# Attention and gated MLP on one core: a third open VectorE exponential, a later read of its scores, and a VectorE queue planned without the drain

## The chip, the cores and the metric

The kernel runs on one core of one Trainium2 chip. The metric is the device time of one execution in microseconds, smaller is better. Three runs of the kernel before took 938.67, 939.95 and 939.96 us; their median is 939.95 us.

## The reference

The input is one sequence of 2048 rows of 640 numbers in bf16. A layer norm without weights is followed by attention with 32 heads of 20 columns, an output projection and a residual sum; then a second layer norm, a gated MLP of width 1728 without a nonlinearity (the gate is multiplied with the up projection), a down projection and another residual sum.

```python
h  = x + A(layernorm(x))
h2 = h + B(layernorm(h))
# A: q, k, v = split(x @ wqkv);  p = softmax(q k^T * 20**-0.5);  (p v) @ wo
# B: ((x @ w_gate) * (x @ w_up)) @ w_down
```

The softmax has 32 x 2048 x 2048 exponentials, and they are the bulk of the work.

## The kernel before

**Units and tiles.** The scores are computed transposed, keys on the 128 partitions and queries along the row. A unit is one head, 128 keys and 512 queries: a 128x512 block of scores, one PSUM bank. Three units make a score tile `sc` of 128x1536 (three banks); there are two such tiles, used in turn. TensorE fills one with three matmuls (line 490), ScalarE takes the exponential of the whole tile into a bf16 tile `E` (line 503), and TensorE multiplies the values with E and sums into `acc` (line 677). Tile i can be filled only when tile i - 2 has been read. There are 683 tiles. Four heads form a group g, 512 queries a pass ("0" to "3"; the last pass is cut in two halves of 256, "A" and "B", for six of its eight groups). One group in one pass is a segment: 64 units, 21.3 tiles. In pass "0" the first four groups are cut in chunks by keys, since keys and values are still being made; all later segments are of the kind "only".

**VectorE's exponentials.** In some tiles ScalarE does only the first 1024 columns, and VectorE computes the exponential of the third unit with four instructions on 128x512: a read of the scores out of PSUM into `xv` (line 528), two polynomial steps into `xt` (lines 537 and 538) and a last step into `xe` (line 533), whose 16-bit integers are the bits of a bf16 number. The first instruction is issued in `emit_x`; the other three go on a list, `x_open`, and are issued one by one wherever the plan sees room on VectorE. A unit is open from its read until its last step. `xv` and `xt` have two buffers each, `xe` has six (X_OUT). A finished unit waits in its `xe` buffer until line 677 has used it; `x_live` counts the units between their read and that use.

**The order of the work is computed while the program is built.** Each engine executes its instructions in the order of the program, so the kernel carries a plan with a clock for each engine in ns: `at["pe"]` for TensorE, `at["exp"]` for the end of ScalarE's last exponential, `at["dve"]` for the time at which VectorE can take another instruction, `at["mi"]` for when the one bank `mi` that all other matmuls share is free, `at["slot"]` for when each score tile is free. A loop over the tiles (line 1206) issues the tile's score matmuls and its exponential (`emit_S`), multiplications with values (`emit_AV`), and then pieces of other jobs (projections, output projection, the MLP) as long as TensorE has time before the next scores are due (`run_job`). If there is no job it issues two matmuls that nobody reads (`keep_warm`, line 463). Every evacuation from PSUM goes through `dve(ns)`, which first lets `spare(ready)` issue waiting VectorE work (steps of open units, layer-norm pieces in `aux`), and then charges ns to `at["dve"]`; ready is `at["pe"]` plus LAT, 150 ns. The charges are about the recorded durations: 690 for a 128x512 evacuation, 490 for 320 columns. A step of an open unit is charged 605, or 720 when the instruction just before it belonged to the same unit. `spare(until)` issues work as long as its cost ends no later than `until` plus TOL, 200 ns.

**Who takes a unit.** `x_takes(i)` (line 514) lets VectorE take the third unit of tile i if the tile is full, lies in one segment of the kind "only" and in a pass before the last (or there are no jobs at all), at least three tiles of the segment follow, fewer than two units are open, `at["dve"]` is less than TOL after `at["pe"]`, and fewer than six units are live. `emit_S` asks only if ScalarE is planned to be busy when the scores are ready. The three conditions at the end are what the change touches:

```python
and len(x_open) < 2 and at["dve"] < at["pe"] + TOL and len(x_live) < X_OUT
```

At the end of a segment `emit_AV` calls `need_x(s)`, which issues all steps still open for that segment before the values of the next one begin. The sum `acc` is then evacuated (line 688), its reciprocal row sums go through DRAM, and GpSimd multiplies (line 600).

Of the kernel before, what the change touches and what calls it, by code (L numbers as in the profile page):

```python
# [11 lines left out]
F32 = mybir.dt.float32  # L12
# [7 lines left out]
P = 128  # L20
# [16 lines left out]
BANK = 512  # L37
# [17 lines left out]
WARM, LEAD = 58, 3  # L55
LAG = 10
EXP_NS, EXP_END, EXP_COL = 50, 166, 5 / 6
S_NS, S_EXP, SWITCH, LAT = 323, 500, 110, 150
TOL, LEAST, MARGIN = 200, 430, 100
WO_NS, SUMS_NS, ROOT_NS, ROWS_NS = 1500, 6000, 5000, 5000  # L60
END_OF_TIME = 10 ** 9
X_LEAST, X_OUT, X_SOON = 3, 6, 4
E_BUFS = 6
SHIFT = 544.0
LOG2E = 1.4426950408889634
# [12 lines left out]
def kernel(  # L78
# [25 lines left out]
    xp = pool("xp")  # L104
# [134 lines left out]
    def dve(ns):  # L239
        ready = at["pe"] + LAT  # L240
        spare(ready)
        x_last[0] = None
        at["dve"] = max(at["dve"], ready) + ns

    def apply1(t, m32, r, k, eng=None):
        eng = eng or nc.vector
# [139 lines left out]
    def step():  # L386
        if cur["fresh"] and (first() or waiting):
            if cur["gen"] is not None:
                jobs.appendleft((cur["key"], cur["gen"]))
            cur["key"], cur["gen"] = (urgent if first() else waiting).popleft()  # L390
        c = advance()
        if c == WAIT:
            waiting.append((cur["key"], cur["gen"]))
            cur["gen"] = None
            c = advance() if jobs and jobs[0][0][0] == "y" else NEXT
        if c is None:
            return None
        if c == FREE:
            advance()
            return FREE  # L400
        if cur["fresh"] and c not in (END, NEXT):
            at["pe"] = max(at["pe"], at["mi"] if cur["key"] != ON_ACC else 0) + SWITCH
        cur["fresh"] = c in (END, NEXT)
        if cur["fresh"]:
            if cur["key"] != ON_ACC:
                at["mi"] = max(at["mi"], at["dve"] + LAT)
        else:
            at["pe"] += c
        return c
# [31 lines left out]
    def spare(until):  # L441
        while True:
            soon = x_open and last_tile[x_open[0][0]] - now["i"] <= X_SOON
            if at["dve"] + (x_next()[0] if soon or x_open and not aux else 600) > until + TOL:
                break
            if soon:
                step_x()
            elif not step_aux() and not step_x():
                break
# [30 lines left out]
    def emit_S(i):  # L480
        sc = scp.tile([P, EW], F32, name="sc")
        us, n = tiles[i]
        for s, kt, j, _ in us:
            p, g = segs[s][0:2]
            ensure(("k", g, kt // TPB))
            ensure(("q", PASS[p][0], g))
        for s, kt, j, o in us:
            p, g = segs[s][0:2]
            b, c0, w = PASS[p]
            nc.tensor.matmul(  # L490
                sc[:, o:o + w],
                lhsT=kT[g][SLOT * j:SLOT * (j + 1), kt * P:(kt + 1) * P],
                rhs=q_of(g, b, c0, w)[SLOT * j:SLOT * (j + 1), :],
                start=True, stop=True)
        begin = max(at["pe"], at["slot"][-2])
        at["pe"] = begin + S_NS
        start = max(at["exp"], begin + S_EXP)
        n_act, took = n, None
        if start == at["exp"] and x_takes(i):
            n_act = n - BANK  # L500
            took = emit_x(sc[:, n_act:n], [(s, kt, j, o - n_act) for s, kt, j, o in us if o >= n_act])
        e = ep.tile([P, EW], BF16, name="E")
        exps = nc.scalar.activation(e[:, 0:n_act], sc[:, 0:n_act], ACT.Exp, bias=EXP_BIAS, scale=SM_SCALE)  # L503
        if took is not None:
            tc.declare_no_dep(exps.ins, took.ins, reason="both only read the score tile, in different banks")
        run = EXP_NS + n_act * EXP_COL
        free = start + run + EXP_END
        at["slot"].append(free if took is None else max(free, at["dve"] + LAT))
        at["exp"] = start + run
        for s, kt, j, o in us:  # L510
            if o < n_act:
                av_q.append((i, s, kt, j, e[:, o:o + PASS[segs[s][0]][2]]))

    def x_takes(i):
        us, n = tiles[i]
        s = us[-1][0]
        return (n == EW and segs[s][4] == "only" and (PASS[segs[s][0]][0] < LAST_B or not jobs and not cur["gen"]) and last_tile[s] - i >= X_LEAST and len({u[0] for u in us}) == 1
                and len(x_open) < 2 and at["dve"] < at["pe"] + TOL and len(x_live) < X_OUT)

    def emit_x(ps, us):  # L520
        s = us[0][0]
        w = PASS[segs[s][0]][2]
        v = xp.tile([P, BANK], F32, name="xv", bufs=2)
        u = v[:].bitcast(U16).rearrange("p (n h) -> p n h", h=2)[:, :, 0]
        t = xp.tile([P, BANK], F32, name="xt", bufs=2)
        e = xp.tile([P, BANK], I16, name="xe", bufs=X_OUT)
        dve(690)
        took = nc.vector.tensor_scalar(v[:], ps, X_SCALE, X_BASE, ALU.mult, ALU.max)  # L528
        x_live.append((s, us[-1][1], us[-1][2]))
        x_left[s] = x_left.get(s, 0) + 1  # L530

        def last():
            nc.vector.scalar_tensor_tensor(e[:], t[:], X_R, v[:], ALU.mult, ALU.add)  # L533
            x_left[s] -= 1
            x_put.append([(now["i"], s, kt, j, e[:, o:o + w].bitcast(BF16)) for s, kt, j, o in us])
        x_open.append((s, deque([
            lambda: nc.vector.scalar_tensor_tensor(t[:], u, X_P, u, ALU.add, ALU.mult),  # L537
            lambda: nc.vector.scalar_tensor_tensor(t[:], t[:], X_Q, u, ALU.add, ALU.mult),  # L538
            last])))
        x_last[0] = x_open[-1]  # L540
        return took
# [103 lines left out]
    def emit_AV(upto):  # L645
        put_x()
        if not av_q:
            return
        if acc["seg"] is not None and av_q[0][1] != acc["seg"]:
            need_x(acc["seg"])  # L650
            put_x()
        s = av_q[0][1]
        p, g, lo, hi, kind = segs[s]
        b, c0, w = PASS[p]
        if acc["seg"] != s:
            if at["pe"] < at["acc"] and now["i"] < acc["from"] and min(u[0] for u in av_q) > now["i"] - E_BUFS:
                return
            acc["seg"], acc["left"], acc["n"] = s, (hi - lo) * HPG, [0] * HPG
            acc["t"] = accp.tile([P, QB], F32, name="acc")
        most, rows = 2 * HPG * QB // w, [[] for _ in range(HPG)]  # L660
        for u in av_q:
            if u[0] > upto or u[1] != s:
                break
            if len(rows[u[3]]) < most // HPG:
                rows[u[3]].append(u)
        ready = sum(len(r) for r in rows)
        if ready < min(most, acc["left"]) and min(u[0] for u in av_q) > upto - 3:
            return
        for u in [r[k] for k in range(most // HPG) for r in rows if k < len(r)]:
            av_q.remove(u)  # L670
            _, _, kt, j, e = u
            x_used.add((s, kt, j))
            while x_live and x_live[0] in x_used:
                x_live.popleft()
            ensure(("v", kt, g // (NG // 2)))
            h = HPG * g + j
            nc.tensor.matmul(  # L677
                acc["t"][SLOT * j:SLOT * (j + 1), 0:w],
                lhsT=vx[kt][:, VS * h:VS * h + SLOT], rhs=e,
                start=(acc["n"][j] == 0), stop=(acc["n"][j] == hi - lo - 1))  # L680
            acc["n"][j] += 1
        acc["left"] -= ready
        at["pe"] += SWITCH + -(-ready // HPG) * w * 5 // 12
        if acc["left"] == 0:
            dve(690)
            if kind in ("copy", "only"):
                asb = parts[g] if kind == "copy" else nrm.tile([P, QB], F32, name="asb")
                nc.vector.tensor_copy(asb[:, 0:w], acc["t"][:, 0:w])
                if kind == "copy":
                    part[g] = asb  # L690
            else:
                asb = part[g]
                nc.vector.tensor_tensor(asb[:, 0:w], acc["t"][:, 0:w], asb[:, 0:w], ALU.add)
            acc["seg"], acc["from"], at["acc"] = None, now["i"] + 2, at["dve"] + LAT
            if s == FINAL:
                final["asb"] = asb
            elif (p, g) in FAST:
                opens["nf", p, g] = at["dve"] + LAT
                urgent.append((("nf", p, g), job_norm(s, asb)))
            elif kind in ("only", "last"):  # L700
                norm(s, asb)
# [640 lines left out]
```

## Time and profile before

| what | value |
|---|---|
| median of three runs | 939.95 us |
| the profiled execution's own time | 938.44 us |
| its span, first to last instruction | 936.4 us |
| granted TensorE clock, mean | 0.993 |
| busy: ScalarE | 887.8 us (95%) |
| busy: TensorE | 818.6 us (87%) |
| busy: VectorE | 620.7 us (66%) |
| busy: GpSimd | 61.6 us (7%) |
| exponentials on ScalarE, 1536 columns | 555, mean 1536 ns |
| exponentials on ScalarE, 1024 columns | 128, mean 1123 ns |
| units on VectorE | 127 |

DVE is VectorE, ACT is ScalarE, PE is TensorE and POOL is GpSimd. A duration is what the profiler records from an instruction's start to its end; on ACT and on DVE the next instruction often starts before the recorded end of the one before, so the number that tells how fast an engine gets on is the distance between two starts. Of the 128 shorter exponentials 127 belong to tiles whose third unit VectorE took; the last is simply the last tile. The waits view lists who stood idle for whom, with the total, the number of times and the longest; an engine can only be late for another one through such a wait.

### The profile page before, as it was taken

How to read it: one execution, taken by the hardware profiler on the slowest of the kernel's cores; microseconds unless marked ns; L12 is line 12 of the kernel's file. 1: busy time of each engine (PE TensorE's matmuls, PEld its weight loads, DVE VectorE, ACT ScalarE, POOL GpSimd, SP SyncE). 2: the span in 40 equal slices, each digit the busy share in tenths (PEclk: the TensorE clock that was granted, in tenths of full speed). 3: DMA queues.
4: the chain of work that ended last, by engine and by line, in shares of the span. 5: the costliest groups of instructions: out<-in, count | busy, mean ns of one | idle time of the engine just before them, and what ended most of it. 6: DMA issues, size and time to landing. Idle time of an engine off the chain costs nothing.

```text
span 936.4 us, 18059 instructions
## 1 busy us (share of the span) xinstructions
PE 818.6 (87%) x7138; PEld 321.7 (34%) x7219; DVE 620.7 (66%) x1222; ACT 887.8 (95%) x719; POOL 61.6 (7%) x155
## 2 busy tenths in 40 slices
PE   8788888888987898998898898998888889978897
PEld 5233232222232222332233222332332334435565
DVE  7674359898888888887888888887562331133342
ACT  6999999999999999999999999999999999999941
POOL 3310011000000000000000000000000000000000
PEclk9999999999999999999999999999899999999999
DMA  6000010011150022014120312002402000212310
GB/s 190 29 2 1 1 27 25 13 35 27 41 164 7 27 77 63 13 34 169 56 57 2 91 48 62 20 29 62 120 2 70 15 12 20 64 28 56 78 43 18
DMA packets 67818, 44.44 MB, mean 47 GB/s; under 512 B 18504, under 2 KB 63404, under 8 KB 67728
## 3 DMA queue, kind: packets, MB, share of 16 engines
q1 hardware_dynamic: 67728, 43.23, 16.6%
q8 instruction: 58, 0.95, 0.4%
q14 instruction: 32, 0.26, 0.1%
HBM read 35.91 MB, written 7.30 MB: 46 GB/s over the span
## 4 chain that ended last, share of the span: by engine, by line
ACT 51%; PE 24%; issue 18%; DVE 7%; ACTq 0%
ACT E L503 51%; PE sc L490 5%; PE acc L677 4%; PE mi L980 3%; PE mi L1035 3%; PE mi L291 2%; PE f L980 2%; PE f L1035 1%; PE mi L305 1%; PE mi L463 1%; DVE xt L538 1%; DVE st L193 1%; DVE u L258 1%; DVE kT L298 1%; PE mi L998 1%
## 5 line engine op out<-in xcount | busy, mean ns | idle before, releaser
L503 ACT ACTIVATE E<-sc 128x1536 bf16<-128x1536 f32 (+1 forms) x683 | 870.3, 1459 | 8.8 <-PE sc L490 6.4
L490 PE MATMUL sc<-qa,kT 32*128 32x512 bf16 x1536 | 201.1, 384 | 47.5 <-ACT E L503 37.0
L490 PEld LDWEIGHTS <-kT 32*128 32x128 bf16 x2432 | 83.8, 91 | 282.8 <-issue 236.1
L677 PE MATMUL acc<-E,vx 128*32 128x512 bf16 (+1 forms) x2305 | 168.2, 351 | 0.5 <-ACT E L503 0.5
L528 DVE TENSOR_SCALAR xv<-sc 128x512 f32<-128x512 f32 x127 | 86.9, 688 | 32.3 <-PE sc L490 31.6
L538 DVE SCALAR_TENSOR_TENSOR xt<-xt,xv 128x512 f32<-128x512 f32 x127 | 92.6, 737 | 0.7
L533 DVE SCALAR_TENSOR_TENSOR xe<-xt,xv 128x512 int16<-128x512 f32 x127 | 90.8, 720 | 0.8
L291 PE MATMUL mi<-lnT,wp 128*128 128x512 bf16 x280 | 81.8, 381 | 10.4 <-DVE kT L298 3.8
L537 DVE SCALAR_TENSOR_TENSOR xt<-xv 128x512 f32<-128x512 uint16 x127 | 87.5, 704 | 0.3
L490 PE MATMUL sc<-qb,kT 32*128 32x256 bf16 (+1 forms) x896 | 69.1, 291 | 16.5 <-ACT E L503 13.3
L600 POOL TENSOR_TENSOR on<-asb,bc 128x512 bf16<-128x512 f32 (+1 forms) x30 | 36.5, 1216 | 694.6 <-DMA bc<-scr 547.7
L677 PEld LDWEIGHTS <-vx 128*32 128x32 bf16 x2432 | 44.4, 95 | 64.3 <-issue 63.8
L1035 PE MATMUL mi<-wd,hh 128*128 128x320 bf16 x364 | 64.3, 302 | 2.0 <-DVE xr L1039 2.0
L258 DVE CAST u<-mi 128x512 bf16<-128x512 f32 (+1 forms) x42 | 29.0, 690 | 36.1 <-PE mi L980 31.7
L1035 PEld LDWEIGHTS <-hh 128*128 128x128 bf16 x448 | 38.4, 97 | 39.9 <-issue 28.3
L980 PE MATMUL mi<-ln2T,wg 128*128 128x512 bf16 (+1 forms) x161 | 45.8, 382 | 6.9 <-DVE u L258 6.4
L463 PE MATMUL mi<-kT,ident 128*128 128x512 bf16 x151 | 48.6, 390 | 1.8 <-issue 0.5
L980 PE MATMUL mi<-ln2T,wu 128*128 128x512 bf16 (+1 forms) x157 | 45.2, 387 | 5.7 <-DVE hh L988 4.7
L988 DVE TENSOR_TENSOR hh<-mi,u 128x512 bf16<-128x512 f32 (+1 forms) x42 | 28.8, 685 | 25.4 <-PE mi L980 22.9
L291 PEld LDWEIGHTS <-wp 128*128 128x128 bf16 x310 | 25.0, 97 | 52.9 <-issue 39.1
L914 PE MATMUL mi<-wo,on 128*128 128x320 bf16 x224 | 38.6, 301 | 2.4 <-DVE xr L918 2.3
L298 DVE TENSOR_SCALAR kT<-mi,one_row 128x512 bf16<-128x512 f32 x30 | 22.4, 746 | 26.7 <-PE mi L291 26.5
(151 smaller groups left out, 582.6 us busy)
## 6 DMA issues: line engine op xcount, KB each, us to landing
bc<-scr SPq DMA_DIRECT2D x100, 64.0 KB
wu<-in_B_w_up_dram SPq DMA_DIRECT2D x20, 320.0 KB
wg<-in_B_w_gate_dram SPq DMA_DIRECT2D x20, 320.0 KB
qsp<-qa SPq DMA_DIRECT2D x8, 384.0 KB
xr<-in_A_x_dram SPq DMA_DIRECT2D x16, 160.0 KB
out_dram<-xr SPq DMA_DIRECT2D x14, 160.0 KB
wd<-in_B_w_down_dram SPq DMA_DIRECT2D x13, 160.0 KB
xs<-in_A_x_dram SPq DMA_DIRECT2D x3, 640.0 KB
```

Source lines behind the costliest of these rows:

```text
L291: nc.tensor.matmul(ps[:], lhsT=wslice(m, g, c), rhs=lnT[:, c, ch * QB:(ch + 1) * QB], start=(c == 0), stop=(c == KT - 1))
L463: nc.tensor.matmul(ps[:], lhsT=ident[:], rhs=kT[0][:, 0:BANK], start=True, stop=True)
L490: nc.tensor.matmul(sc[:, o:o + w], lhsT=kT[g][SLOT * j:SLOT * (j + 1), kt * P:(kt + 1) * P], rhs=q_of(g, b, c0, w)[SLOT * j:SLOT * (j + 1) ...
L503: exps = nc.scalar.activation(e[:, 0:n_act], sc[:, 0:n_act], ACT.Exp, bias=EXP_BIAS, scale=SM_SCALE)
L528: took = nc.vector.tensor_scalar(v[:], ps, X_SCALE, X_BASE, ALU.mult, ALU.max)
L533: nc.vector.scalar_tensor_tensor(e[:], t[:], X_R, v[:], ALU.mult, ALU.add)
L537: lambda: nc.vector.scalar_tensor_tensor(t[:], u, X_P, u, ALU.add, ALU.mult),
L538: lambda: nc.vector.scalar_tensor_tensor(t[:], t[:], X_Q, u, ALU.add, ALU.mult),
L677: nc.tensor.matmul(acc["t"][SLOT * j:SLOT * (j + 1), 0:w], lhsT=vx[kt][:, VS * h:VS * h + SLOT], rhs=e, start=(acc["n"][j] == 0), stop=(ac ...
L914: nc.tensor.matmul(ps[:, 0:HALF], lhsT=on[g][:, t * P:(t + 1) * P], rhs=wo[g][:, cs], start=(g == 0), stop=(g == NG - 1))
L980: nc.tensor.matmul(ps[0:M, 0:n], lhsT=st["w", fp][k][:, c, f2 * P:f2 * P + M], rhs=st["ln2T"][:, c, c0:c0 + n], start=(c == 0), stop=(c == ...
L1035: nc.tensor.matmul(ps[:, 0:HALF], lhsT=st["hh"][f][0:K, t * P:(t + 1) * P], rhs=late["Wd"][f][0:K, cs], start=(f == 0), stop=(f == 2 * FP ...
```

## The change

Five edits. (1) A constant DRAIN of 80 ns: `dve(ns)` charges 80 ns less to `at["dve"]`, and the places that use `at["dve"]` as the time when a result is there (for `mi`, for the score tile, for `acc`) add it back. (2) A third unit may be open, and `xv` and `xt` get a third buffer. (3) `xe` has five buffers in place of six, and at most four live units let another one be taken. (4) A new time `last_of_x`, the planned start of the tile's shortened exponential plus 50 + 1024 x 5/6 + 166 - 150 - 690 - 200, that is about 29 ns after the start: a unit may be taken if `at["dve"]` is less than that (or less than `at["pe"]` plus TOL, as before). (5) Before the unit is taken, `spare(last_of_x)` issues waiting VectorE work up to that time, so that the read of the scores stands behind it in VectorE's queue.

```diff
--- before.py
+++ after.py
@@ -55,11 +55,12 @@
 WARM, LEAD = 58, 3
 LAG = 10
 EXP_NS, EXP_END, EXP_COL = 50, 166, 5 / 6
-S_NS, S_EXP, SWITCH, LAT = 323, 500, 110, 150
+S_NS, S_EXP, SWITCH, LAT, DRAIN = 323, 500, 110, 150, 80
 TOL, LEAST, MARGIN = 200, 430, 100
 WO_NS, SUMS_NS, ROOT_NS, ROWS_NS = 1500, 6000, 5000, 5000
 END_OF_TIME = 10 ** 9
-X_LEAST, X_OUT, X_SOON = 3, 6, 4
+X_LEAST, X_OUT, X_SOON = 3, 5, 4
+X_READ, X_SLACK = 690, 200
 E_BUFS = 6
 SHIFT = 544.0
 LOG2E = 1.4426950408889634
@@ -240,7 +241,7 @@
         ready = at["pe"] + LAT
         spare(ready)
         x_last[0] = None
-        at["dve"] = max(at["dve"], ready) + ns
+        at["dve"] = max(at["dve"], ready) + ns - DRAIN
 
     def apply1(t, m32, r, k, eng=None):
         eng = eng or nc.vector
@@ -403,7 +404,7 @@
         cur["fresh"] = c in (END, NEXT)
         if cur["fresh"]:
             if cur["key"] != ON_ACC:
-                at["mi"] = max(at["mi"], at["dve"] + LAT)
+                at["mi"] = max(at["mi"], at["dve"] + DRAIN + LAT)
         else:
             at["pe"] += c
         return c
@@ -496,8 +497,10 @@
         at["pe"] = begin + S_NS
         start = max(at["exp"], begin + S_EXP)
         n_act, took = n, None
-        if start == at["exp"] and x_takes(i):
+        last_of_x = start + EXP_NS + (n - BANK) * EXP_COL + EXP_END - LAT - X_READ - X_SLACK
+        if start == at["exp"] and x_takes(i, last_of_x):
             n_act = n - BANK
+            spare(last_of_x)
             took = emit_x(sc[:, n_act:n], [(s, kt, j, o - n_act) for s, kt, j, o in us if o >= n_act])
         e = ep.tile([P, EW], BF16, name="E")
         exps = nc.scalar.activation(e[:, 0:n_act], sc[:, 0:n_act], ACT.Exp, bias=EXP_BIAS, scale=SM_SCALE)
@@ -505,26 +508,26 @@
             tc.declare_no_dep(exps.ins, took.ins, reason="both only read the score tile, in different banks")
         run = EXP_NS + n_act * EXP_COL
         free = start + run + EXP_END
-        at["slot"].append(free if took is None else max(free, at["dve"] + LAT))
+        at["slot"].append(free if took is None else max(free, at["dve"] + DRAIN + LAT))
         at["exp"] = start + run
         for s, kt, j, o in us:
             if o < n_act:
                 av_q.append((i, s, kt, j, e[:, o:o + PASS[segs[s][0]][2]]))
 
-    def x_takes(i):
+    def x_takes(i, last):
         us, n = tiles[i]
         s = us[-1][0]
         return (n == EW and segs[s][4] == "only" and (PASS[segs[s][0]][0] < LAST_B or not jobs and not cur["gen"]) and last_tile[s] - i >= X_LEAST and len({u[0] for u in us}) == 1
-                and len(x_open) < 2 and at["dve"] < at["pe"] + TOL and len(x_live) < X_OUT)
+                and len(x_open) < 3 and at["dve"] < max(last, at["pe"] + TOL) and len(x_live) < X_OUT)
 
     def emit_x(ps, us):
         s = us[0][0]
         w = PASS[segs[s][0]][2]
-        v = xp.tile([P, BANK], F32, name="xv", bufs=2)
+        v = xp.tile([P, BANK], F32, name="xv", bufs=3)
         u = v[:].bitcast(U16).rearrange("p (n h) -> p n h", h=2)[:, :, 0]
-        t = xp.tile([P, BANK], F32, name="xt", bufs=2)
+        t = xp.tile([P, BANK], F32, name="xt", bufs=3)
         e = xp.tile([P, BANK], I16, name="xe", bufs=X_OUT)
-        dve(690)
+        dve(X_READ)
         took = nc.vector.tensor_scalar(v[:], ps, X_SCALE, X_BASE, ALU.mult, ALU.max)
         x_live.append((s, us[-1][1], us[-1][2]))
         x_left[s] = x_left.get(s, 0) + 1
@@ -691,11 +694,11 @@
             else:
                 asb = part[g]
                 nc.vector.tensor_tensor(asb[:, 0:w], acc["t"][:, 0:w], asb[:, 0:w], ALU.add)
-            acc["seg"], acc["from"], at["acc"] = None, now["i"] + 2, at["dve"] + LAT
+            acc["seg"], acc["from"], at["acc"] = None, now["i"] + 2, at["dve"] + DRAIN + LAT
             if s == FINAL:
                 final["asb"] = asb
             elif (p, g) in FAST:
-                opens["nf", p, g] = at["dve"] + LAT
+                opens["nf", p, g] = at["dve"] + DRAIN + LAT
                 urgent.append((("nf", p, g), job_norm(s, asb)))
             elif kind in ("only", "last"):
                 norm(s, asb)
```

## Prediction

> **What bounds the kernel now.** I read the page first: the busy line, the 40 slices, the chain of waits.
>
> ```profile
> PE 818.6 (87%) x7138; PEld 321.7 (34%) x7219; DVE 620.7 (66%) x1222; ACT 887.8 (95%) x719; POOL 61.6 (7%) x155
> ...
> DVE  7674359898888888887888888887562331133342
> ACT  6999999999999999999999999999999999999941
> ...
> ACT 51%; PE 24%; issue 18%; DVE 7%; ACTq 0%
> ```
>
> ScalarE is full from the second slice to the 38th. VectorE is at seven to nine tenths in slices 7 to 28; that is where it takes units. I then asked for busy time in four stretches, cut at the starts of exponentials 86 and 512 and at the last one's end; columns are the stretch, PE, PEld, DVE, ACT and POOL busy (count), clock and DMA.
>
> ```profile
> 133.80:661.20 527.40, 466.54 (x3554) 153.76 (x3604) 450.99 (x793) 522.84 (x427) 31.33 (x22) 1.00 0.19 53
> 661.20:894.10 232.90, 203.77 (x2386) 93.52 (x2403) 76.71 (x204) 231.15 (x172) 9.07 (x11) 0.99 0.15 41
> 894.10:936.40 42.30, 35.27 (x285) 26.35 (x284) 16.46 (x49) 9.93 (x25) 0.00 (x0) 0.97 0.12 34
> ```
>
> The first stretch is the one that the change can move: 125 of the 127 units lie in it. VectorE is idle for 527.4 - 451.0 = 76.4 us of it. TensorE spends 38.5 us of its busy time there on the matmuls of line 463 that nobody reads, so it has room. The other stretches hold two units and the same jobs as before; I cost the edits there at nothing.
>
> **The price of one unit.** Counting starts of exponentials in the stretch, 1536 columns most often take 1.330 us to the next start and 1024 columns 0.904: **a unit taken saves ScalarE 0.426 us**. The stretch would take 301 x 1.330 + 125 x 0.904 = 513.3 us at that pace and takes 527.4, so 14.1 us are lost to late scores, in many small pieces.
>
> What a unit costs VectorE is read from its timeline (start, duration):
>
> ```profile
> 619.60 0.63 DVE L538 SCALAR_TENSOR_TENSOR xt<-xt,xv 128x512 f32<-128x512 f32 x1
> 620.14 0.68 DVE L537 SCALAR_TENSOR_TENSOR xt<-xv 128x512 f32<-128x512 uint16 x1
> 620.74 0.68 DVE L533 SCALAR_TENSOR_TENSOR xe<-xt,xv 128x512 int16<-128x512 f32 x1
> 621.34 0.68 DVE L538 SCALAR_TENSOR_TENSOR xt<-xt,xv 128x512 f32<-128x512 f32 x1
> 622.05 0.69 DVE L533 SCALAR_TENSOR_TENSOR xe<-xt,xv 128x512 int16<-128x512 f32 x1
> 622.74 0.69 DVE L528 TENSOR_SCALAR xv<-sc 128x512 f32<-128x512 f32 x1
> 623.35 0.48 DVE L1039 TENSOR_TENSOR xr<-mi,xr 128x320 bf16<-128x320 f32 x1
> ...
> 632.50 0.69 DVE L533 SCALAR_TENSOR_TENSOR xe<-xt,xv 128x512 int16<-128x512 f32 x1
> ...
> 636.04 0.69 DVE L528 TENSOR_SCALAR xv<-sc 128x512 f32<-128x512 f32 x1 [2.85 <-PE sc L490]
> ```
>
> Starts stand 0.60 apart, 0.70 where a step needs the one just before it, and each record overlaps the next by 0.08. Read and three steps: 0.60 + 3 x 0.63 = 2.5 us. The last two rows show idle time at the end of a segment: both open units are done, no tile may be taken, VectorE waits 2.85 us.
>
> **Part by part.**
>
> DRAIN. The plan charges 690 for an evacuation after which the next instruction starts 604 ns later (mean of 93 reads with the next right behind). The stretch has 287 VectorE instructions that read PSUM and 21 reciprocals, all charged this way: 308 x 0.08 = 24.6 us in which the plan thinks VectorE busy and it isn't. Nothing is added to the program; steps and reads are issued earlier into that time. The release times get the 80 ns back. What the Trainium skill says here, on "VectorE: DVE Perf Modes", section "The DRAIN you can't avoid", is the opposite of what the edit assumes: the next operation doesn't start until the pipe has emptied. With the recorded end taken for that moment, the rows disagree by 80 ns; by the page the edit would be worth nothing or less (rival 4), by the rows 24.6 us of VectorE.
>
> Third open unit and later read. By the timeline, of the 76.4 us idle, 21.1 stand before a read with nothing open and 11.2 before a read with one open; the waits view gives the bulk:
>
> ```profile
> DVE xv L528 <- PE sc L490: 31.6, 54, 2.8
> ...
> PE sc L490 <- DVE xv L528: 1.9, 5, 0.9
> ```
>
> A read placed behind steps, up to the tile's exponential, finds its scores there; a third unit leaves up to four more instructions, 2.5 us, for the segment's end, where the first row's long waits are. The other 44.1 us are short waits of evacuations for TensorE (u, xr, qa, hh), most with two units open: there the plan had no step issued though time was there.
>
> How much of it is filled can't be read from the trace. Bounds: nothing (below nothing there is no reason: no unit is taken away unless the five buffers do it, rival 3), and all 76.4. A unit more costs 2.5 us and shortens the stretch by 0.43, so all of it would be 76.4 / 2.93 = 26 units, 11.1 us. I take six tenths of the waits before reads (19 us), since tiles early in a segment still have nothing behind them, and half of the rest (22 us), about what the 24.6 us of false charges buy: 41 / 2.93 = **14 units, 14 x 0.426 = 6.0 us less**. Tiles are not short: 366 of the stretch qualify by place, 125 are taken, and at 151 of the 241 others two units were open half a microsecond before the exponential's start.
>
> Five `xe` in place of six. A unit lives 10.6 us on average from its read to its use (10.2 median); counted at the qualifying tiles, four were live at 44 of 366, never more. With three open this grows by one at most; it binds at times and costs a unit or two, within the guess.
>
> More steps per wait. The late read is the one new danger: score tile i + 2 now waits for whichever comes last, ScalarE or the read. Before, the read ended a median 0.56 us ahead of the exponential and behind it in 8 of 125. The edit plans the end 0.2 us before ScalarE gives the tile back, up to TOL later. After that the scores of i + 2 have 1.33 - 0.5 - 0.17 = 0.66 us to spare (scores 0.5 before their exponential, 0.17 to give the tile back), or 0.24 if tile i + 1 is taken too. Queued behind a read on VectorE are evacuations of `mi`; TensorE's next job waits for them, and the next scores behind that job. Bounds for all this: 14.1 us less (every loss now present gone, which a truer plan could only begin) and 11.2 us more (rival 2). I take **1.5 us more**, since the 11 latest reads of before were followed by a loss of only 26 ns at tile i + 2, 12 to 28 after early ones.
>
> Sum: 938.44 - 6.0 + 1.5 = 933.9 in terms of the profiled execution, whose time is 1.5 us under the median of the runs. Against the median: 939.95 - 4.5 = **935.4 us**.
>
> **Rivals.**
>
> 1. Full packing. Nearly all idle time is filled, 22 to 26 units, and the truer plan loses no more: 9.4 to 11.1 us, 929 to 930.5. For it: many tiles to choose from, false charges gone. Against: each of the 20 segments ends with four tiles that may not be taken.
>
> 2. Slower: a full VectorE hands its lateness on. Where GpSimd multiplies, a step of a unit is held up, and it goes through to ScalarE:
>
> ```profile
> 572.62 1.34 POOL L600 TENSOR_TENSOR on<-asb,bc 128x512 bf16<-128x512 f32 x1 [25.79 <-DMA bc<-scr]
> 572.75 1.75 DVE L538 SCALAR_TENSOR_TENSOR xt<-xt,xv 128x512 f32<-128x512 f32 x1
> ...
> 574.43 0.68 DVE L988 TENSOR_TENSOR hh<-mi,u 128x512 bf16<-128x512 f32 x1
> ...
> 575.16 0.81 PE L980 MATMUL mi<-ln2T,wu 128*128 128x512 bf16 x3 [1.31 <-DVE hh L988]
> ...
> 576.39 3.28 ACT L503 ACTIVATE E<-sc 128x1024 bf16<-128x1024 f32 x3 [0.77 <-PE sc L490]
> ```
>
> 18 steps of the stretch last over 0.9 us, 14.2 us over their usual 0.72 together. The Trainium skill explains the row ("SBUF — State Buffer", "SBUF: two separate sides"): a VectorE operation with two SBUF inputs and a GpSimd one lock each other out. The plan doesn't know of it. Today idle time behind each absorbs most: within 3 us of these 18, ScalarE loses 3.0 us. Without idle time, and with late reads, up to 14.2 - 3.0 = 11.2 us more reach it. Against 6.0 gained that is 5 us slower, 945. It turns the sign once over 9.0 of the 14.2 arrive, that is when most delays pass the 0.2 us of the plan and the 0.24 to 0.66 us behind it.
>
> 3. No more units. The limit of live units, or idle time that the plan can't foresee since TensorE is late, eats the third unit, or the gain is lost in equal stalls: 0 to 4 units, 0 to 1.7 us less, stalls the same size: 938 to 941.
>
> 4. The next VectorE instruction waits for the recorded end. Then 24.6 us are over-promised, 1.2 us in each of 20 segments, of which some 0.66 are covered: 11 us on ScalarE less 6.0, 5 us slower, 945. This is the page's rule above; the overlapping starts speak against it.
>
> **How the numbers follow.** The forecast, with 6 to 20 units and 0 to 3 us of stalls, 931 to 938: 0.58. Rival 1: 0.11. Rival 3: 0.16. Rival 2: 0.13. Rival 4: 0.02. The range, 929.5 to 941.5, leaves out rivals 2 and 4 and little of rival 1. A measurement of this kernel can tell 0.2%, 1.9 us: faster takes the forecast, all but a little of it, rival 1 and a little of rival 3: 0.70; the same, 938.1 to 941.8: 0.15; slower: 0.15.
>
> **What would show it.** Right: exponentials of 1024 columns go from 128 to about 142; VectorE's idle time in the stretch falls from 76 to 30 to 45 us; its waits for `sc` fall below 15 us; the time from one start to the next stays 0.60; ScalarE's loss against its pace stays near 14 to 16 us. Wrong: as many units as before (rival 3), the waits of `sc` for `xv` and of `mi` for VectorE up by more than the units save (rival 2), or a longer stretch after 661 us, which I hold at 232.9 + 42.3.

## The result, and the profile after

The changed kernel takes 945.99 us (median of 6 runs, 942.88 to 949.61) against 939.01 us for the kernel before on the same chip: a ratio of **1.0077, 95% interval 1.0051 to 1.0102. It is slower**, and outside the predicted range of 929.5 to 941.5. Its profiled execution took 945.31 us, its span is 943.5.

The page after, busy line, VectorE's slices and the chain of waits:

```profile
PE 824.7 (87%) x7173; PEld 320.3 (34%) x7173; DVE 666.6 (71%) x1314; ACT 881.5 (93%) x719; POOL 61.4 (7%) x155
...
DVE  7674358998998999999998999999563231133242
...
ACT 37%; PE 27%; DVE 20%; issue 15%; DMA 1%; ACTq 0%; DVEq 0%
```

VectorE did take more units, 150 in place of 127, and ScalarE is busy 6 us less. But VectorE is now 20% of the chain that ended last, in place of 7%, and ScalarE's share fell from 51 to 37%. The stretches, cut at the same exponentials as before (columns as in the prediction):

```profile
134.60:665.90 531.30, 467.10 (x3558) 150.50 (x3557) 495.20 (x882) 516.18 (x428) 30.89 (x22) 0.99 0.19 52
665.90:901.50 235.60, 207.93 (x2401) 94.55 (x2400) 78.87 (x207) 231.01 (x172) 9.06 (x11) 0.98 0.15 41
```

Between exponentials 86 and 512, which I go on calling the stretch, there are 147 units, 22 more. At ScalarE's pace (1.330 and 0.904 us) that is 504.0 us in place of 513.3, **9.3 us less**. It takes 531.3 in place of 527.4. The loss against the pace went from 14.1 to 27.3 us, **13.2 us more**. The last pass is 2.7 us longer, the part ahead of the stretch 0.8. VectorE idles 36.1 us in the stretch in place of 76.4. The waits of the whole execution, from the three engines' views:

```profile
DVE xv L531 <- PE sc L491: 4.9, 6, 1.5
...
PE sc L491 <- DVE xv L531: 13.6, 21, 1.9
...
ACT E L506 <- PE sc L491: 15.8, 35, 1.3
...
ACT E L506 <- PE acc L680: 4.0, 5, 1.7
```

The first pair has changed places: VectorE's reads used to wait for scores (31.6 us, now 4.9), now scores wait for reads (1.9 us, now 13.6). ScalarE's waits for scores were 6.4 us and are 15.8 (in the stretch 3.1 and 9.8). The last line, waits for `E` tiles that TensorE has not yet multiplied into `acc`, didn't exist before.

**A late read, as it looks in the timeline** (start, duration; the first lines are VectorE's):

```profile
150.75 0.68 DVE L541 SCALAR_TENSOR_TENSOR xt<-xt,xv 128x512 f32<-128x512 f32 x1
...
151.35 0.68 DVE L540 SCALAR_TENSOR_TENSOR xt<-xv 128x512 f32<-128x512 uint16 x1
...
151.95 0.68 DVE L531 TENSOR_SCALAR xv<-sc 128x512 f32<-128x512 f32 x1
...
152.69 0.39 PE L491 MATMUL sc<-qa,kT 32*128 32x512 bf16 x3 [0.50 <-DVE xv L531]
153.19 1.45 ACT L506 ACTIVATE E<-sc 128x1536 bf16<-128x1536 f32 x1 [0.20 <-PE sc L491]
```

VectorE works without a gap, 0.60 us from start to start, and its read comes behind two steps. The scores of the tile after next can start only when it is over, and ScalarE runs dry. In the stretch 46 of 147 reads now end behind their exponential (8 of 125 before), 23 by over 0.3 us (2 before). At the tile after next those 23 are followed by a loss of 226 ns on average, 5.2 us together; reads more than half a microsecond ahead by 7 ns. Of the 23, 19 have a step that was slowed beside GpSimd ahead of them in the same run of VectorE without a gap of over 0.15 us; of all 147 reads 55 have. The one shown is among the four that don't.

**The clock.** The third thing that is new is how long TensorE's granted clock is low. It falls to 0.50 for 3.4 us or a multiple of it; until the last exponential this happened for 10.2 us before and 20.5 after. Two windows of 3.4 us each around two of the falls, and the window ahead of a third (the clock is the third number from the end):

```profile
183.00:186.40 3.40, 1.51 (x12) 0.51 (x10) 3.40 (x6) 3.19 (x4) 0.00 (x0) 1.00 0.00 0
186.40:189.80 3.40, 3.40 (x18) 0.65 (x16) 2.56 (x5) 2.18 (x2) 0.00 (x0) 0.50 0.00 0
285.40:288.80 3.40, 1.36 (x16) 0.40 (x14) 2.16 (x5) 2.63 (x3) 0.00 (x0) 1.00 0.03 3
288.80:292.20 3.40, 3.36 (x15) 1.34 (x13) 2.70 (x6) 1.51 (x2) 0.00 (x0) 0.50 0.26 77
...
667.60:671.00 3.40, 2.57 (x25) 1.50 (x24) 3.37 (x9) 3.40 (x4) 0.00 (x0) 1.00 0.98 287
```

Ahead of the first two falls TensorE is busy 1.51 and 1.36 of the 3.4 us (it waited for `xv`), then runs at half clock. ScalarE loses 2.0 us in the first fall and the 2 us behind it. In the second it loses 3.2, of which 1.7 stand at the exponential that the wait itself made late. So these waits are paid twice. But the third fall came after 2.57 us of work. I counted the windows of all 20 profiles from 30 us on, in steps of 3.41 us from each profile's first fall, leaving out those that begin at half clock. All 20 windows in which TensorE was busy less than half the time were followed by a fall, 54 of 195 with 50 to 70%, and 22 of 4685 with more. A long wait brings a fall; not every fall comes from one.

**A wait for a transfer.** The read ahead of the second fall, the latest of all (1.95 us behind its exponential), was held up by neither GpSimd nor a full queue (SPq issues the transfers):

```profile
272.38 9.22 SPq L893 DMA_DIRECT2D wd<-in_B_w_down_dram  x14
...
274.61 0.68 DVE L691 COPY asb<-acc 128x512 f32<-128x512 f32 x1
...
281.70 0.52 SPq L581 DMA_DIRECT2D sums<-asb  x1
...
286.64 0.25 DVE L592 RECIPROCAL ri<-sums_all 128x16 f32<-128x16 f32 x1 [2.45 <-DMA sums_all<-sums]
```

A segment's row sums, evacuated at 274.61, go out at 281.70, behind fourteen loads of `wd` in the same queue. The plan puts the reciprocal 6 us or more after the evacuation (SUMS_NS); it stands in front of the steps and the read, and VectorE waits 2.45 us for the sums. From there to 6 us behind the reciprocal ScalarE loses 3.2 us, the same that are named at the second fall. Before the change no reciprocal of the stretch waited. The same wait, 2.0 to 4.6 us long, stands in the profiles of e2, e3, e5, e11 and e15, with 2.9 to 5.5 us lost behind it; e14 has one of 0.8 us that costs nothing, and the other runs have none.

### The profile page after: what moved, and what is told of

Same layout as the page of the kernel before. It is cut to its first block, busy times and chain, and to the rows that moved or that the text cites. A ratio compares the mean times of both kernels' runs of the same rounds, so it can differ in the third digit from the quotient of the medians.

```text
span 943.5 us, 18139 instructions
## 1 busy us (share of the span) xinstructions
PE 824.7 (87%) x7173; PEld 320.3 (34%) x7173; DVE 666.6 (71%) x1314; ACT 881.5 (93%) x719; POOL 61.4 (7%) x155
## 4 chain that ended last, share of the span: by engine, by line
ACT 37%; PE 27%; DVE 20%; issue 15%; DMA 1%; ACTq 0%; DVEq 0%
ACT E L506 37%; PE sc L491 6%; PE acc L680 4%; PE mi L983 4%; DVE xt L540 3%; DVE xe L536 3%; DVE xt L541 3%; DVE xv L531 3%; PE mi L1038 2%; PE mi L292 2%; PE mi L306 2%; PE f L983 2%; PE mi L1001 2%; DVE st L194 1%; PE f L1038 1%
## 5 line engine op out<-in xcount | busy, mean ns | idle before, releaser
L506 ACT ACTIVATE E<-sc 128x1536 bf16<-128x1536 f32 (+1 forms) x683 | 864.0, 1408 | 22.5 <-PE sc L491 15.8
L491 PEld LDWEIGHTS <-kT 32*128 32x128 bf16 x2432 | 81.7, 91 | 293.7 <-issue 222.3
L540 DVE SCALAR_TENSOR_TENSOR xt<-xv 128x512 f32<-128x512 uint16 x150 | 106.5, 722 | 0.3
L541 DVE SCALAR_TENSOR_TENSOR xt<-xt,xv 128x512 f32<-128x512 f32 x150 | 105.4, 711 | 0.3
L531 DVE TENSOR_SCALAR xv<-sc 128x512 f32<-128x512 f32 x150 | 100.9, 680 | 5.3 <-PE sc L491 4.9
L536 DVE SCALAR_TENSOR_TENSOR xe<-xt,xv 128x512 int16<-128x512 f32 x150 | 103.9, 698 | 0.3
L292 PE MATMUL mi<-lnT,wp 128*128 128x512 bf16 x305 | 83.8, 384 | 4.8 <-DVE qa L299 1.9
L680 PE MATMUL acc<-xe,vx 128*32 128x512 bf16 x150 | 48.1, 386 | 0.0
L917 PE MATMUL mi<-wo,on 128*128 128x320 bf16 x224 | 41.6, 313 | 2.4 <-DVE xr L921 2.3
L464 PE MATMUL mi<-kT,ident 128*128 128x512 bf16 x132 | 41.1, 394 | 1.9 <-DVE ln2T L259 1.2
```

What stands on the lines that cost most here:

```text
L292: nc.tensor.matmul(ps[:], lhsT=wslice(m, g, c), rhs=lnT[:, c, ch * QB:(ch + 1) * QB], start=(c == 0), stop=(c == KT - 1))
L464: nc.tensor.matmul(ps[:], lhsT=ident[:], rhs=kT[0][:, 0:BANK], start=True, stop=True)
L491: nc.tensor.matmul(sc[:, o:o + w], lhsT=kT[g][SLOT * j:SLOT * (j + 1), kt * P:(kt + 1) * P], rhs=q_of(g, b, c0, w)[SLOT * j:SLOT * (j + 1) ...
L680: nc.tensor.matmul(acc["t"][SLOT * j:SLOT * (j + 1), 0:w], lhsT=vx[kt][:, VS * h:VS * h + SLOT], rhs=e, start=(acc["n"][j] == 0), stop=(ac ...
L917: nc.tensor.matmul(ps[:, 0:HALF], lhsT=on[g][:, t * P:(t + 1) * P], rhs=wo[g][:, cs], start=(g == 0), stop=(g == NG - 1))
```

## The experiments

Where nothing else is said, the edit is to the changed kernel; times are medians beside runs of the kernel before on the same chip (938.95 to 939.84 us), ratios are to it and are what to compare between runs. Units are all of a kernel, the loss is that of the stretch in its profiled execution.

**First four: undo one part.** The theories A, B and C are named in the first expectation, the later ones where they first appear.

e1, edits 4 and 5 undone:

```diff
-            spare(last_of_x)
...
-                and len(x_open) < 3 and at["dve"] < max(last, at["pe"] + TOL) and len(x_live) < X_OUT)
+                and len(x_open) < 3 and at["dve"] < at["pe"] + TOL and len(x_live) < X_OUT)
```

> The changed kernel without edits 4 and 5: a unit's scores are read as early as before; three may be open and the plan leaves out the drain. The program holds 142 units. Theory A (VectorE is full, and every delay that the plan doesn't know reaches ScalarE, whichever edit filled it): the loss of ScalarE in the stretch between exponentials 86 and 512 stays at 20 us or more (27.3 with the change, 14.1 before), and the time is 0.2 to 0.5% above the kernel before. Theory B (the late read alone did it, since it used up the slack of the score tiles): the loss is back at some 14 us, and with 14 units more than before the time is some 0.6% below the kernel before. Theory C (the third open unit delays the end of a segment, acc is late, E runs out): the waits of ScalarE's exponential for acc stay at some 4 us, the time 0.2 to 0.4% above.

949.58 us, **1.0125** (1.0104 to 1.0145). Loss 26.2 us, although 9 reads in place of 46 end late and TensorE's waits for `xv` are 5.4 us. ScalarE's waits for `acc` are 6.6 us in the stretch. B falls: the late read isn't what costs most.

e2, two open (`xv` and `xt` go back to two buffers as well; `xe` keeps five):

```diff
-                and len(x_open) < 3 and ...
+                and len(x_open) < 2 and ...
```

> The changed kernel with two units open at most and two buffers of xv and xt, as before; late read and the plan without the drain stay. The program holds 139 units. A: VectorE's idle time in the stretch rises from 36 to some 60 us, the loss falls to some 18 us, the time is within 0.2% of the kernel before. B: the reads stay as late, the loss stays over 22 us, 0.3% above. C: ScalarE's waits for acc (4.0 us in the stretch) go to nothing and with them 4 to 5 us of loss, the rest stays: 0.1 to 0.3% above.

946.26 us, **1.0088** (1.0059 to 1.0116). The waits for `acc` are gone, as C has it; VectorE idles 57.7 us and the loss falls to 20.6, as A has it. But the time is above what any of the three expected: the last pass takes 239.3 us, 6.4 more than before, with three units in it in place of two. And 4.1 us of the loss stand behind the reciprocal's wait.

e3, the drain stays in the plan:

```diff
-S_NS, S_EXP, SWITCH, LAT, DRAIN = 323, 500, 110, 150, 80
+S_NS, S_EXP, SWITCH, LAT, DRAIN = 323, 500, 110, 150, 0
```

> The changed kernel with DRAIN set to 0: three open, late read, but the plan again charges every read of PSUM 80 ns too much. The program holds 142 units. A: the 80 ns are a hidden reserve of some 25 us in the stretch that takes up the delays; the loss falls to some 15 us and the time is 0.3 to 0.6% below the kernel before. B and C: reads are as late and segments end as late in the plan, the loss stays over 22 us, and the time is 0.2 to 0.4% above.

954.56 us, **1.0170** (1.0147 to 1.0192), the slowest of these, with VectorE idle 70.5 us. A falls as the whole story: with reserve in plenty the loss is 38.8 us. Waits of ScalarE for `acc` are 10.4 us of it, 2.9 us stand behind the reciprocal's wait, and the clock is at half for 37.5 us of the stretch. One segment's end in its timeline:

```profile
392.29 0.39 PE L680 MATMUL acc<-xe,vx 128*32 128x512 bf16 x1
392.29 0.68 DVE L536 SCALAR_TENSOR_TENSOR xe<-xt,xv 128x512 int16<-128x512 f32 x1
392.89 0.68 DVE L691 COPY asb<-acc 128x512 f32<-128x512 f32 x1
...
393.62 0.62 PE L680 MATMUL acc<-E,vx 128*32 128x512 bf16 x8 [0.95 <-DVE asb L691]
394.12 4.86 ACT L506 ACTIVATE E<-sc 128x1024 bf16<-128x1024 f32 x4 [2.35 <-PE acc L680]
```

The segment's last unit is multiplied, a step of the next unit stands ahead of the evacuation of `acc`, TensorE waits 0.95 us for it, and ScalarE, which has filled all six `E` tiles, stands 2.35 us for one to come free. Its last pass takes 232.3 us, as before the change, so what e2 lost there may have come with edit 1 (e7 and e14 test it).

e4, no hold-ups (steps of a unit that a GpSimd multiplication slows) any more, since VectorE multiplies itself:

```diff
-                nc.gpsimd.tensor_tensor(On[g][:, c0:c0 + w], asb[:, 0:w], bc[:, 0:w], ALU.mult)
+                dve(690 * w // QB)
+                nc.vector.tensor_tensor(On[g][:, c0:c0 + w], asb[:, 0:w], bc[:, 0:w], ALU.mult)
```

> The changed kernel with the multiplication of line 600 moved from GpSimd to VectorE and charged to the plan like an evacuation, so that no step of a unit is held up by GpSimd. The program holds 147 units. If those hold-ups (17 instructions over 0.9 us in the stretch, 13.9 us over their usual length) are the delays that reach ScalarE, the loss falls from 27 to 15 to 18 us and the time is 0.2 to 0.5% below the kernel before. If the delays come from anywhere else (the late read by itself, the plan's drift, the segment's end), the loss stays over 23 us and the time 0.5% or more above.

948.64 us, **1.0109** (1.0090 to 1.0128). Its waits:

```profile
ACT E L506 <- PE acc L681: 10.1, 5, 3.5
...
PE sc L491 <- DVE xv L531: 2.4, 5, 0.8
```

The scores' waits for reads are nearly gone (13.6 us to 2.4) and reads over 0.3 us late fall from 23 to 3, although VectorE has the 22 multiplications of the stretch to do as well. So most of the late reads came from the hold-ups. The loss is still 27.4: the waits at segments' ends went from 4.0 to 10.1 us, and the clock is at half for 23.9 us of the stretch in place of 10.2.

**Next four: pairs of causes, and single edits.** e5, e2 and e4 together:

> The changed kernel with two open units (as in the second run, where ScalarE's waits for acc were gone) and with the multiplication of line 600 on VectorE, in the plan (as in the fourth run, where the late reads were gone). The program holds 138 units. Theory D (two separate waits do the harm: a read that a VectorE step beside GpSimd has delayed, and a segment's end that the third unit delays until E runs out; and each long enough wait of TensorE also halves its clock for 3.4 us or more): with both gone the loss in the stretch is at most 15 us, there are no more than two dips of the clock in it, and the time is 0.2 to 0.6% below the kernel before. Theory E (any denser packing of VectorE makes TensorE and ScalarE late, in whatever way is left): the loss stays over 19 us and the time is above the kernel before.

940.68 us, **1.0022** (1.0009 to 1.0035), 5.6 us better than e2. Loss 14.8 us, no waits for `acc`, 1.7 us for `xv`: theory D holds in the stretch, which takes 524.3 us, 3.1 less than before; 4.1 of the 14.8 us stand behind the reciprocal's wait. The last pass takes 238.9. So the time is above the kernel before, as E has it, but not where E looks for it. Six falls of the clock came until the last exponential, three in the stretch, one more than D expected.

e6, no unit taken in a segment's last five tiles, in place of the last three:

```diff
-X_LEAST, X_OUT, X_SOON = 3, 5, 4
+X_LEAST, X_OUT, X_SOON = 5, 5, 4
```

> The changed kernel with three open units, but none taken in the last five tiles of a segment in place of the last three (X_LEAST 5). The program holds 142 units. D: ScalarE's waits for acc (4.0 us in the stretch with the change, 6.6 to 10 in the runs with 142 to 147 units and three open) go to under 1 us, the late reads stay: loss 18 to 22 us, time 0.2 to 0.6% above the kernel before. If the wait for acc comes from three open units anywhere, not from the segment's end, it stays at 4 us or more.

940.86 us, **1.0025** (1.0014 to 1.0037): 5.1 us less than with the change, with 8 units fewer, no waits for `acc`, loss 20.8. Of the late reads half stay (12 by over 0.3 us, waits for `xv` 8.2 us). As D expected.

e7, the kernel before with edit 1 alone (DRAIN 80):

> The kernel before with edit 1 alone: the plan leaves out the drain; two open, early read, six xe. The program holds 131 units. D: neither wait has its cause here, reads stay early, the loss is within 2 us of 14 and the time 0.1 to 0.3% below the kernel before. E, or the theory that the 80 ns are a reserve that the delays need: loss 17 us or more, time at or above the kernel before.

944.63 us, **1.0062** (1.0048 to 1.0076). The stretch is harmless, 527.1 us with loss 15.1, so neither text was right: the last pass takes 238.5 us, 5.6 more.

e8, the kernel before with edits 4 and 5 alone:

> The kernel before with edits 4 and 5 alone: late read, two open, six xe, the plan with the drain. The program holds 132 units. D: reads behind the exponential's end rise from 8 to some 25, TensorE's waits of sc for xv from 1.9 to some 6 us; loss 17 to 20 us, no waits for acc, time 0 to 0.3% above the kernel before. If the late read is harmless by itself: loss 14, time 0.2 to 0.3% below.

936.45 us, **0.9965** (0.9952 to 0.9979): faster. Loss 13.9, 14 reads late, 3.8 us of waits for `xv`. That is D's rival, nearly to the number: the late read by itself is a gain.

**The third edit alone, the pairs, and the clock.** e9, the kernel before with edits 2 and 3 alone:

> The kernel before with edits 2 and 3 alone: three open, five xe, early read, the plan with the drain. The program holds 136 units. Theory D (the third unit delays the segment's end, E runs out): ScalarE's waits for acc of 5 us or more in the stretch, loss over 22 us, time 0.5% or more above the kernel before. If the third unit does harm only with a late read or a plan without the drain: loss 15, no waits for acc, time 0.2 to 0.4% below.

948.12 us, **1.0089** (1.0071 to 1.0108). Waits of ScalarE for `acc` 7.4 us, loss 24.9, last pass 232.0. Three open units do their harm without the other edits, at the segment's end. That it isn't the five `xe` buffers is shown by e2 and e6, which have five and no such waits.

e10, e7 with one charge mended. In e7's last pass the same small stall, 0.30 to 0.32 us, comes back at tiles 649, 655, 657, 659, 661, 666 and 670, where the MLP's pairs run:

```profile
861.10 0.42 DVE L1005 TENSOR_TENSOR hh<-mi,u 128x256 bf16<-128x256 f32 x1
...
861.58 0.92 PE L998 MATMUL mi<-ln2T,qa 128*128 128x256 bf16 x7 [0.64 <-DVE hh L1005]
```

The pair's evacuations start 0.46 us apart, the second needs the first, so nothing overlaps; edit 1 takes 80 ns off both and gives back one. The plan believes `mi` free too early, TensorE stands 0.64 us in front of it with the next scores queued behind.

```diff
-                    dve(330)
+                    dve(330 + DRAIN)
```

> Edit 1 alone as in the seventh run, but the first of the two chained charges of the small MLP's pairs (330 ns for 256 columns, whose two evacuations start 0.46 us apart, with no overlap to take off) gets its 80 ns back. The program holds the same 131 units. Theory F (edit 1's loss lies in the last pass, since the plan believes the bank mi free 80 ns too early in every pair, puts a job ahead of the scores and TensorE waits): the stalls of some 0.32 us at tiles 649 to 671 go, the last pass's stretch shrinks from 238.5 to 233 to 236 us, and the time comes down from 0.6% above the kernel before to within 0.2% of it. Rival: edit 1 does its harm as a lost reserve everywhere, or by dips of the clock that happen to fall there: 0.4% or more above still.

943.32 us, **1.0041** (1.0026 to 1.0056). All but one of those stalls are gone, the last pass takes 235.7 us. The ratio fell by 0.0021, some 2.0 us of the 5.8 that edit 1 cost in e7, though the two intervals overlap; F holds for the mechanism and not for its size.

e11, e5 with the pairs mended the same way:

> The fifth run's kernel (late read, plan without the drain, two open, line 600's multiplication on VectorE) with the pairs' charge mended as in the tenth. The program holds 138 units. If the three causes found (late reads beside GpSimd, the segment's end, the pairs' charge) are all there is, the stretch stays at some 524 us, the last pass comes down from 239 to 233 to 236, and the time is 0.2 to 0.5% below the kernel before. If the clock's dips come with any denser order, they stay at six or more and the time stays at or above the kernel before.

937.58 us, **0.9988** (0.9972 to 1.0003): 3.1 us less than e5, the last pass 236.5, less of a gain than expected. The reciprocal's wait (4.0 us lost behind it) is still there.

e12, the kernel before without the filler matmuls:

```diff
-        for _ in range(2):
+        for _ in range(0):
             nc.tensor.matmul(ps[:], lhsT=ident[:], rhs=kT[0][:, 0:BANK], start=True, stop=True)
```

> The kernel before without the matmuls of line 463 that nobody reads (keep_warm issues none; the plan still counts their time); nothing else is changed, and no result depends on them. It measures the clock by itself. If TensorE's clock falls to half whenever TensorE has been idle for a large part of some 3.4 us, the dips rise from three to fifteen or more, with no other wait added, and the time goes up by 1% or more. If dips have to do with load or heat, they don't rise and the time is the same or less.

956.36 us, **1.0176** (1.0156 to 1.0197). The clock, in 40 slices:

```profile
PEclk9999999999987999995597999995588999969999
```

In the stretch it is at half for 114 us, in place of 3.4, and the loss is 23.9 us, in place of 14.1, with not one unit or wait added by design. It was less work for TensorE, not more, that brought the clock down.

**Edit 1 in place, and the causes taken away.** e13 and e14 split e7: `DRAIN if 86 <= now["i"] < 512 else 0`, and the reverse.

> Edit 1 alone, and only while tiles 86 to 511 are planned, the stretch in which VectorE takes units; before and after it the plan charges as before. The program holds 130 units. Theory G (edit 1's harm lies outside the stretch, where it gives nothing): the last pass's stretch is back at 233 us and the time is 0.1 to 0.3% below the kernel before. Rival (a lost reserve where VectorE is full): the harm stays, 0.3% or more above.

> Edit 1 alone, only outside tiles 86 to 511. The program holds 128 units. Theory G: nearly all the harm of edit 1 is here, 0.4 to 0.7% above the kernel before, with the last pass's stretch at 235 to 239 us. Rival: within 0.2%.

e13: 941.21 us, **1.0014** (1.0003 to 1.0025). e14: 941.83 us, **1.0025** (1.0013 to 1.0037), last pass 238.0. Each has a part; inside, three more units bring 1.3 us and the loss takes 1.8. Neither expectation is met fully: outside costs less than G said, inside isn't a gain.

e15, e5 with edit 1 only inside the stretch; e16, e15 with three open and X_LEAST 5:

> Late read, plan without the drain only inside tiles 86 to 511, two units open, line 600's multiplication on VectorE. The program holds 136 units. If the causes found are all: stretch 523 to 525 us, last pass 233, the time 0.4 to 0.6% below the kernel before. If something else of the change does harm as well: within 0.2% or above.

> As the run before with three units open, but none taken in the last five tiles of a segment. The program holds 140 units. If the third unit's only fault is the segment's end: no waits for acc, loss in the stretch 13 to 16 us, the time 0.4 to 0.8% below the kernel before. If a third open unit costs in another way: loss over 18 us, the time within 0.2% or above.

e15: 937.14 us, **0.9980** (0.9967 to 0.9994), half of what was expected or less (stretch 522.5 us, last pass 235.6). The causes found so far were not all: in its profile the reciprocal waits 4.6 us for row sums, and 5.5 of the 13.0 us of loss stand behind that. e16: **933.05 us, 0.9934** (0.9919 to 0.9949), faster than both kernels and than all the others. It has neither waits for `acc` nor a reciprocal that waits, so its 4.1 us against e15 are not all the third unit's (four units more are 1.7 us):

```profile
ACT E L509 <- PE sc L494: 13.0, 24, 1.9
...
PE sc L494 <- DVE xv L534: 3.6, 7, 0.9
```

Its profiled execution is the slowest of its six (938.11 us, with the clock at half for 27 us of the stretch), so its loss of 18.2 us is no measure of the others.

e17, e16 with the multiplication on GpSimd again; e18, e16 with DRAIN 0:

> The sixteenth run's kernel (late read, three open, none taken in a segment's last five tiles, plan without the drain inside tiles 86 to 511 only), with the multiplication of line 600 on GpSimd again. The program holds 142 units. If steps held up beside GpSimd make the reads late and cost by themselves: reads over 0.3 us behind the exponential go from 3 back to 10 or more, TensorE's waits for xv from 3.6 to 8 us or more, the time 0.3 to 0.7% above the sixteenth run. If not: within 0.2% of it.

> The sixteenth run's kernel with DRAIN 0 everywhere. The program holds 130 units, ten fewer. If planning without the drain is worth its units in the mended kernel: about 10 x 0.426 = 4.3 us of ScalarE's pace more, less what the loss falls: 0.2 to 0.4% above the sixteenth run. If the 80 ns are a reserve worth as much as the units: the same time as the sixteenth.

e17: 939.40 us, **1.0000** (0.9983 to 1.0016). Reads over 0.3 us late are 13 (3 in e16), the waits for `xv` 8.6 us, and nine of the 13 have a slowed step ahead of them in the same run of VectorE (23 of all 139). So the hold-ups, with what they set off, cost some 6 us. e18: 936.86 us, **0.9971** (0.9954 to 0.9988): ten units fewer, 3.8 us slower. In the mended kernel edit 1 is worth its units.

## Why the prediction was wrong, point by point

1. **The units.** "14 units, 6.0 us less" was too little: 22 units in the stretch, 9.3 us, near the bound of 26. The price of a unit held, and so did the start-to-start time: 0.601 us behind a read (127 reads) against 0.604 before. Rival 4, VectorE's next start at the recorded end, is out. The rule that it leaned on, in the Trainium skill's "VectorE: DVE Perf Modes", section "The DRAIN you can't avoid", is qualified in that section itself: an operation that isn't held starts earlier. The trace agrees, since records still overlap by some 0.08 us.

2. **The stalls, the step that turned the sign.** "I take 1.5 us more" was the mis-sized term; it measured 13.2. I took it from the 11 latest reads of before, and those were hardly late: none by more than 0.45 us, eight by 0.13 us or not at all, against 23 by 0.32 to 1.95 us with the change. A full VectorE passes delays on: e4 against the change and e17 against e16 show the hold-ups beside GpSimd doing it. Rival 2 described this. That its 945 is near the 946.0 is in part luck: it isn't the whole cause, since e4 took its delays away and was no faster. Of the 13.2 us, 3.2 stand behind the reciprocal's wait for the row sums, which no rival named; no run takes that wait away alone.

3. **The segment's end, a step with the wrong sign.** "A third unit leaves up to four more instructions, 2.5 us, for the segment's end" was booked as work for an idle engine. Those steps stand ahead of the end of the sum, and ScalarE has six `E` tiles until then. e9 shows it alone (7.4 us of waits for `acc`, 0.9% slower), e2 and e6 show it gone. The plan doesn't count `E` tiles, and neither did I.

4. **"The other stretches ... at nothing".** Wrong by 3.5 us in the profile (0.8 ahead, 2.7 in the last pass). Edit 1 costs something there: e14 is 0.25% slower with it outside the stretch alone. How much of the 3.5 us that is isn't shown, since single profiles scatter: the part ahead took 134.4 us in e13 too, whose plan is that of before up to tile 86, and the last pass 232.0 to 235.6 without edit 1 in it (e12 left out), 235.1 to 239.3 with it. One mechanism is shown, the pairs' charge, worth some 2.0 us of e7's 5.8.

5. **The clock**, not in the sum at all, though the kernel has matmuls that nobody reads. A wait that left TensorE less than half of 3.4 us of work was followed by half clock each time (20 windows of 20). The Trainium skill, "TensorE: Matmul & The Clock Gate", section "Part 1: The HAM clock gate (the "warmup" mystery)", gives the rule: half clock after at least one idle window of about 3.4 us. The 3.4 us and the half agree with the rows; but here no window ahead of a fall was wholly idle, and 1.36, 1.51 and even 2.57 us of work did not prevent one.

6. **The edits don't add.** Late read alone 0.9965, third unit alone 1.0089, edit 1 alone 1.0062; third unit and late read 1.0170 (e3), all three 1.0077. In e3 the waits for `acc` are 10.4 us, with all three 4.0; that edit 1 lets steps go earlier and so clears segments sooner is my reading and was not tried alone.

The forecast's own corner, 6 units with 3 us of stalls, would have been 940.4 and not 938; that changes neither its range nor its sign.

What stays open: the rest of edit 1's loss (0.1 to 0.4% in e10, e13 and e14), and what the reciprocal's wait costs by itself. Falls of the clock are part of it in the profiles, but their length changes by itself (e7 and e10, whose programs agree until the pairs, fall for 3.4 us at 509 and 6.8 at 666, and for 6.8 at 507 and 3.4 at 667), and only one execution of each was profiled. That the change's runs scatter more (6.7 us over six, 2.6 for six of before) may come from the same; that wasn't shown.

## What to carry to other kernels

An engine that is planned full hands every delay that the plan doesn't know to the engine that it serves, so look for those delays (another engine that slows a step, a chained pair, a small number of buffers, a transfer behind others in its queue) before filling its idle time: filling the same idle time cost 0.8% or gave 0.7%, depending on such places. Follow each added instruction to what stands behind it in its queue, above all where one sum ends and the next begins. And count what an added wait does to TensorE's clock, not only the wait.

## What the runs showed of the hardware

TensorE's granted clock halved in steps of 3.4 us, after each of the 20 windows in which TensorE had been busy less than half of 3.4 us, and at times after fuller ones. Without the filler matmuls it was at half for 114 us of one stretch (e12): 178 matmuls with no reader (by their weight loads; 151 of the matmuls were recorded) are worth 1.8% here. A VectorE step with two SBUF inputs that meets a GpSimd multiplication still takes up to 1.76 us in place of 0.7, and moving that multiplication to VectorE separates e16 from e17 by 6 us.
